# Score matmuls of the first two batches read queries from the transpose buffer, with less bias, and loads and mixing in a new order

## The chip, the cores and the metric

The kernel runs on one core of a Trainium2 chip. The metric is device time in microseconds (us) of one execution. The profile adds a trace of one execution, whose span is about 2 us shorter than the time of the same execution. Engine names are those of the profile: PE is TensorE, PEld its weight loads, DVE is VectorE, ACT is ScalarE, POOL is GpSimd and SP is SyncE.

## The reference, cut to what matters

```python
# batch 8, heads 8, sequence 576, head_dim 64, 8 global tokens, window 32
scores = scale * (q @ k.T)
mask   = (abs(i - j) <= 32) | is_global[i] | is_global[j]
x      = softmax(where(mask, scores, -1e9)) @ v          # heads side by side: [B, 576, 512]
h      = relu(x.T @ w_tok1) @ w_tok2                     # token mixer, 576 -> 256 -> 576
u      = x + h.T
out    = u + relu(u @ w_ch1) @ w_ch2                     # channel mixer, 512 -> 1536 -> 512
```

Each batch therefore goes through scores, exponentials, the rows of the global tokens ("og" in the kernel), the banded product with V ("pv"), the token mixer ("a1p", "hp") and the two channel matmuls ("b1p", "op"). The channel mixer is most of the work of PE.

## The kernel before

K and Q of four heads arrive as 32-row blocks. DVE transposes them into `kcs` and `qcs`, in natural order of the tokens. A copy then spreads each into a layout with one block for each tile of 128 tokens, with 8 columns of the global tokens ahead of each block of queries. The score matmuls read that second layout. In batches 0 and 1 the band mask is added by matmuls of a bias (`biasm`) into the same PSUM tile. Later batches multiply the exponentials by a 0/1 mask (`bandm`) on DVE.

```python
def Xq(b, hg):                       # transpose into natural order
    nc.vector.transpose(out=qcs[hg][:, 0:S]..., in_=st[b]["q16"]...[:, hg]...)

def Xc(b, hg, eng):                  # the copy of Q into blocks with the global columns
    o = qTs[b % 2][:, hg].rearrange("p (t x) -> p t x", t=NT)[:, :, NG:QS]
    copy(eng, o, qcs[hg].rearrange("p (t x) -> p t x", t=NT))

def S_mm0(b, hg, part, rp, ps):      # one score tile: 2 heads
    qf, kT = q16s[b][:, hg], k16s[b][:, hg]
    for i in range(2):
        for off, c0, n in B_SEG[part]:                    # bias
            nc.tensor.matmul(ps[:, i, off:off+n], lhsT=identS, rhs=biasm[:, c0:c0+n], start=(off == 0), stop=False)
    for off, kc, lo, n in S_SEG[part]:                    # 16 matmuls of Q and K
        for e in range(2):
            for i in range(2):
                rs = slice(32 * (2 * rp + i), 32 * (2 * rp + i) + 32)
                nc.tensor.matmul(ps[:, i, off:off+n], lhsT=kT[rs, kc:kc+P, e], rhs=qf[rs, lo:lo+n, e], ...)

# V of batch 0: one block v16 that DVE transposes, four side pieces, and a copy shifted by 32 rows
def load_v0(): ...                                        # v16, 4 transfers
def Xv0(): ...                                            # transpose v16 into vsh
def dup_v(b):
    nc.sync.dma_start(out=vsh[b % 2][32:P, NT:NC], in_=vsh[b % 2][0:P - 32, 2:NT])

def OG(b, get):                                           # rows of the global tokens
    for c in range(NC):
        for r in range(4):
            nc.tensor.matmul(ps[...], lhsT=egs[b % 2][:, c, r], rhs=V[:, c, r::4, :], ...)
    ...                                                   # DVE writes the rows back into V

# --- order of the prologue (cut) ---
eg_const(0); load_v0(); Xk(0, 1); Kc(0, 1, nc.gpsimd)
load_qk(1, (0,)); Xq(0, 1); Xc(0, 1, nc.gpsimd); glob0(1); load_qk(1, (1,))
load_v(0, (0, 5, 6, 7), False)                            # side pieces of V
...
Xv0(); dup_v(0); nc.sync.dma_start(out=vsh[1][0:32, 0:NT], in_=vsh[0][0:32, 0:NT])
...
rest = OG(0, psv)
Xc(1, 0, nc.vector)
S1(0, 0, 0); S1(0, 0, 1); n0 = PV(0, 0, psd); ...         # all four tiles of batch 1, heads 0-3
X1(0, 1, nc.scalar)                                       # K of batch 1, heads 4-7, copied by ScalarE

# --- batch 0: what is mixed with its two channel layers D4 and D5 ---
A = [(0.7, lambda: M2(0, 2, psv))] + s1 + ... + gap(0.8)
A += phase_og(1)[:1] + gap(1.7) + phase_og(1)[1:] + M1u(1)
merge(A, D4[2:])
merge(G(2) + m[:1] + ... + x2[:2] + ... + s2[:1] + x2[2:] + ... + s2[1:] + gap(1.5), D5)
```

`merge` interleaves the pieces of a list with the channel groups by their estimated cost; `gap` holds a place for some microseconds; `fill` puts matmuls on zeros into PE's queue.

The softmax here doesn't subtract the row's maximum and nothing guards it: scores larger than these inputs give would overflow.

Of the kernel before, what the change touches and what calls it, by code (L numbers as in the profile page):

```python
# [17 lines left out]
P = 128  # L18
# [13 lines left out]
B_SEG = (((0, 0, 136), (136, 208, 200), (336, 440, 104), (440, 1088, 72)), ((0, 544, 136), (136, 712, 240), (376, 984, 104)))  # L32
LAG_S = 2
# [3 lines left out]
FILL = (14, 18, 0, 4, 5, 0)  # L37
# [3 lines left out]
def kernel(  # L41
# [236 lines left out]
    def S_mm0(b, hg, part, rp, ps):  # L278
        qf, kT = q16s[b][:, hg], k16s[b][:, hg]
        for i in range(2):  # L280
            for off, c0, n in B_SEG[part]:
                nc.tensor.matmul(
                    ps[:, i, off : off + n], lhsT=identS, rhs=biasm[:, c0 : c0 + n], start=(off == 0), stop=False,
                )
        for off, kc, lo, n in S_SEG[part]:
            for e in range(2):
                for i in range(2):
                    r = 2 * rp + i
                    rs = slice(32 * r, 32 * r + 32)
                    nc.tensor.matmul(  # L290
                        ps[:, i, off : off + n], lhsT=kT[rs, kc : kc + P, e], rhs=qf[rs, lo : lo + n, e],
                        start=False, stop=(e == 1 and off == S_SEG[part][-1][0]),
                    )
# [25 lines left out]
    def S_mask(b, hg, rs=range(4)):  # L319
        for r in rs:  # L320
            eh = e_all[:, 4 * hg + r]
            nc.vector.tensor_mul(out=eh, in0=eh, in1=bandm)  # L322
# [309 lines left out]
    load_qk(0, (1,))  # L632
# [18 lines left out]

    zero_e(e0)
# [4 lines left out]
    zeros(kT3[1].bitcast(F16).rearrange("p g (t x) -> p g t x", t=NT)[:, :, 1:NT, 0 : 2 * WIN])  # L657
    zeros(vsh[0][0:32, 0, :, 0:D])
    zeros(x16s[0][LAST:P, NT - 1])
    zeros(x16s[1][0:LAST, NT - 1])  # L660
# [30 lines left out]
    nc.vector.tensor_scalar(out=ident, in0=it_f[:, 0:P], scalar1=pf, scalar2=None, op0=ALU.is_equal)  # L691
    gidx_f = const.tile([P, NG], F32)
# [5 lines left out]
    for hg in range(2):  # L698
        gather(gq, q, 0, (hg,))
        gather(gk, k, 0, (hg,))  # L700
# [6 lines left out]
    rown, pad = [const.tile([P, NC + 3], F32, name=n) for n in ("rown", "pad")]  # L707
    nc.vector.tensor_scalar(out=pad, in0=kpos, scalar1=-500.0, scalar2=NEG, op0=ALU.is_lt, op1=ALU.mult)
# [4 lines left out]
    nc.vector.tensor_scalar(out=identS, in0=it_f[:, 0:P], scalar1=pf, scalar2=sc, op0=ALU.is_equal, op1=ALU.mult)  # L713

    hgp = int_op("hgp", 4, ALU.logical_shift_right, 1, ALU.bitwise_and)
    nc.vector.tensor_scalar(out=dsel, in0=it8[:, 0:2], scalar1=hgp, scalar2=None, op0=ALU.is_equal)
# [6 lines left out]
    def mask_glob(c0, n):  # L723
        nc.vector.tensor_scalar(
            out=win(biasm[0:32, EB * c0 + 8 : EB * c0 + 8 + P], EB, n),
            in0=it_f[0:32, P * c0 : P * (c0 + n)].rearrange("p (t x) -> p t x", x=P),
            scalar1=gppm[0:32], scalar2=hm1[0:32], op0=ALU.is_equal, op1=ALU.add,
        )
# [5 lines left out]
    mask_rows(EB + 168, 96, 0, 8)  # L734
    Xq(0, 0)
    Xk(0, 0)
    for t, o, x0 in ((qcs, qTs[0][:, 0].rearrange("p (t x) -> p t x", t=NT), NG), (kcs, kT3[0][:, 0].rearrange("p (t x) -> p t x", t=NT), WIN)):
        nc.scalar.copy(out=o[:, :, x0:].bitcast(F16), in_=t[0].rearrange("p (t x) -> p t x", t=NT).bitcast(F16))
    mask_glob(0, 2)
    nc.vector.tensor_scalar(  # L740
        out=biasm[0:32, 4 * EB + 8 : 4 * EB + 72], in0=it_f[0:32, 4 * P : S],
        scalar1=gppm[0:32], scalar2=hm1[0:32], op0=ALU.is_equal, op1=ALU.add,
    )
# [4 lines left out]
    )  # L748
    nc.vector.tensor_mul(out=gd, in0=gd, in1=gd)
    nc.vector.tensor_scalar(out=gd, in0=gd, scalar1=1024.5, scalar2=NEG, op0=ALU.is_lt, op1=ALU.mult)  # L750
    for c0, b0, n in ((0, 0, NT), (NT, 2 * EB - NG, NC - NT)):
# [3 lines left out]
        )  # L755
    def eg_const(i):
# [3 lines left out]
    def glob0(hg):  # L760
        gather_t(gq, gqT, 0, slice(hg, hg + 1))
        globals_(0, nc.vector, (hg,))
        gather_t(gk, gkT, 0, slice(hg, hg + 1))
        for part in (1, 0):
            globals_k(0, nc.vector, part, slice(hg, hg + 1))

    zeros(w1l[LAST:P, 0])
    zeros(w1l[0:LAST, 1])
    zeros(w2[:, :, S:])
    glob0(0)  # L770
    for b0, z0, w, c0 in ((2 * EB + 8, 64, P, 2), (2 * EB + 168, 0, 96, 9)):
        nc.vector.tensor_tensor(
            out=win(biasm[:, b0 : b0 + w], EB, 2), in0=nb[:, z0 : z0 + w].unsqueeze(1).to_broadcast([P, 2, w]),
            in1=rown[:, c0 : c0 + 2].unsqueeze(2).to_broadcast([P, 2, w]), op=ALU.add,
        )
    mask_glob(2, 2)
    eg_const(0)
    load_v0()
    Xk(0, 1)
    Kc(0, 1, nc.gpsimd)  # L780
    load_qk(1, (0,))
    Xq(0, 1)
    Xc(0, 1, nc.gpsimd)
    glob0(1)
    load_qk(1, (1,))
    load_v(0, (0, 5, 6, 7), False)
    nc.gpsimd.dma_start(out=w1, in_=moe_w_tok1[0 : S - LAST, :].rearrange("(c p) x -> p c x", p=P))
    for i in range(2):
# [11 lines left out]
    for n in range(4):  # L800
# [5 lines left out]
        if n == 0:  # L806
            zero_e(e_all)
# [170 lines left out]
```

## Time and profile before

The time was 331.89 us, median of two runs (331.49 to 332.29). The profile is of one more execution, of 329.62 us, with a span of 327.8 us at a mean clock of 0.971 (1 is full speed).

A single tile of the trace marks each stage. "M4" is the first full-width matmul of batch 0's first channel layer.

| landmark | before, us |
|---|---|
| og of batch 0 ends | 30.55 |
| first matmul of the token mixer's second half | 46.66 |
| M4 | 55.16 |
| og of batch 2 starts | 97.49 |
| og of batch 3 starts | 134.22 |
| end of the last matmul | 322.82 |

The parts of the profile that bound the kernel are shown in the prediction below. In PE's timeline, a line gives start, duration, engine, source line, operation, output and inputs, sizes and count, and in brackets the idle time before it with what ended it. This is the start of the token mixer's second half in the kernel before:

```profile
46.66 0.38 PE L579 MATMUL hp_0b<-a,w 128*128 128x512 f16 x1 [1.90 <-ACT a L865]
```

PE stands for 1.90 us until ScalarE has done a ReLU, and 0.35 us more for the other half, which DVE does.

### The profile page before, as it was taken

The numbers are of one execution on the slowest core, as the hardware profiler recorded it, in microseconds if no ns is written. First come the engines' busy times: TensorE is split into PE (matmuls) and PEld (weight loads), VectorE is DVE, ScalarE is ACT, GpSimd is POOL, SyncE is SP. The second block draws the span as 40 slices with busy tenths as digits, with TensorE's granted clock in tenths as the row PEclk, the third lists the DMA queues.
The fourth block names the chain that finished last, engine by engine and source line by source line (L and its number), as shares of the span: only waits on it lengthen the run. The fifth ranks groups of instructions, "written<-read, shape, count | busy, mean of one in ns | idle before, by whom it ended". The sixth has DMA issues, their size and how long they took to land.

```text
span 327.8 us, 7740 instructions
## 1 busy us (share of the span) xinstructions
PE 299.3 (91%) x3194; PEld 160.7 (49%) x3194; DVE 188.3 (57%) x361; ACT 154.9 (47%) x310; POOL 112.0 (34%) x215
## 2 busy tenths in 40 slices
PE   8852967998989999999999999999999999999993
PEld 3542834663435644554445644544456445444641
DVE  7964365266755748595758376757664766151021
ACT  8880434740654555346544562556346535404600
POOL 8865570001588827421732156124312000000000
PEclk9995699999799999999999999999999999999998
DMA  6699999304399999962997069807910251072022
GB/s 120 91 160 176 172 177 203 70 0 98 64 157 168 101 206 111 149 159 59 119 145 146 2 114 143 225 2 123 139 61 2 64 131 32 0 123 87 2 83 77
DMA packets 68290, 34.92 MB, mean 107 GB/s; under 512 B 54656, under 2 KB 58624, under 8 KB 68256
## 3 DMA queue, kind: packets, MB, share of 16 engines
q0 software_dynamic: 44960, 18.19, 47.5%
q1 hardware_dynamic: 23296, 16.25, 19.0%
q8 instruction: 25, 0.41, 0.5%
q14 instruction: 9, 0.07, 0.1%
HBM read 36.38 MB, written 9.44 MB: 140 GB/s over the span
## 4 chain that ended last, share of the span: by engine, by line
PE 69%; DVE 11%; DMA 6%; POOL 6%; issue 3%; ACT 3%; POOLq 0%; DVEq 0%
PE op L478 22%; PE b1p L452 22%; PE s L273 4%; PE hp L411 4%; PE a1p L395 4%; DVE e_all L322 4%; DMA vsh<-in_v_dram 3%; PE pv L370 3%; DMA q<-in_q_dram 3%; PE b1lp L465 2%; PE pv L373 2%; ACT e_all L303 2%; PE s L290 2%; PE og L338 1%; DVE kc L227 1%
## 5 line engine op out<-in xcount | busy, mean ns | idle before, releaser
L452 PE MATMUL b1p<-uT,wc 128*128 128x512 f16 x376 | 91.7, 379 | 2.8 <-DVE osb L482 1.0
L617 ACT ACTIVATE big<-b1p 128x512 f16<-128x512 f32 x95 | 56.6, 598 | 78.3 <-PE b1p L452 76.1
L478 PE MATMUL op<-big 128*128 128x512 f16 x384 | 92.8, 383 | 0.0
L303 ACT ACTIVATE e_all<-s 128x544 f16<-128x544 f32 (+3 forms) x140 | 58.9, 515 | 52.1 <-PE s L273 37.5
L478 PEld LDWEIGHTS <-big 128*128 128x128 f16 x384 | 35.7, 98 | 40.9 <-issue 1.0
L452 PEld LDWEIGHTS <-wc 128*128 128x128 f16 x376 | 33.4, 97 | 40.2 <-issue 7.0
L117 POOL DMA_DIRECT2D vsh<-in_v_dram x60 | 41.7, 713 | 5.8 <-DMA wc<-in_moe_w_ch_dram 3.7
L322 DVE TENSOR_TENSOR e_all<-e_all,bandm 128x1160 f16<-128x1160 f16 x48 | 33.8, 762 | 14.2 <-ACT e_all L303 14.2
L416 DVE TENSOR_TENSOR u<-x,hp 128x1024 f16<-128x1024 f16 x14 | 17.1, 1220 | 34.2 <-PE hp L411 34.2
L482 DVE TENSOR_TENSOR osb<-u,op 128x512 f32<-128x512 f16 x32 | 21.9, 684 | 25.3 <-PE op L478 25.2
L240 POOL COPY kT<-kc 128x640 int32<-128x640 int32 x13 | 9.4, 723 | 78.3 <-DVE kc L227 42.2
L382 DVE TENSOR_TENSOR x<-pv,rr 128x512 f16<-128x512 f32 (+1 forms) x40 | 27.6, 691 | 1.5
L328 POOL COPY eg<-e_all 128x160 f16<-128x160 f16 (+1 forms) x24 | 7.4, 339 | 55.9 <-DVE e_all L322 55.9
L370 PEld LDWEIGHTS <-e_all 128*128 128x128 f16 (+1 forms) x280 | 18.0, 98 | 5.2 <-issue 1.3
L227 DVE STREAM_TRANSPOSE kc<-k 128x576 int32<-128x576 int32 x16 | 19.9, 1244 | 0.4 <-DMA k<-in_k_dram 0.4
L370 PE MATMUL pv<-vsh,e_all 128*128 128x66 f16 (+1 forms) x280 | 20.0, 193 | 0.0
L233 DVE STREAM_TRANSPOSE qc<-q 128x576 int32<-128x576 int32 x16 | 19.8, 1237 | 0.0
L411 PE MATMUL hp<-a,w 128*128 128x512 f16 x72 | 19.1, 379 | 0.6 <-DVE u L416 0.6
L273 PEld LDWEIGHTS <-kT 32*128 32x128 f16 x768 | 12.6, 94 | 14.1 <-issue 11.2
L344 DVE TENSOR_TENSOR vsh<-og,dsel 32x132 f16<-32x132 f32 x32 | 9.2, 288 | 17.6 <-PE og L338 17.2
L381 DVE RECIPROCAL rr<-pv 128x8 f32<-128x8 f32 (+1 forms) x40 | 7.9, 198 | 19.7 <-PE pv L373 16.0
L273 PE MATMUL s<-qT,kT 32*128 32x104 f16 (+3 forms) x768 | 16.3, 218 | 3.1 <-POOL qT L240 2.3
(150 smaller groups left out, 330.3 us busy)
## 6 DMA issues: line engine op xcount, KB each, us to landing
out_dram<-osb SPq DMA_DIRECT2D x32, 256.0 KB, 2.6
k<-in_k_dram POOLq DMA_DIRECT2D x16, 288.0 KB, 9.2
q<-in_q_dram POOLq DMA_DIRECT2D x16, 288.0 KB, 8.2
vsh<-in_v_dram POOLq DMA_DIRECT2D x36, 96.0 KB, 5.5
vsh<-vsh SPq DMA_DIRECT2D x8, 297.0 KB, 6.5
wc<-in_moe_w_ch_dram POOLq DMA_DIRECT2D x3, 512.0 KB, 7.0
big<-in_moe_w_ch_dram POOLq DMA_DIRECT2D x3, 512.0 KB
out_dram<-osb SPq DMA_DIRECT2D x8, 128.0 KB, 5.8
```

The lines of the kernel that those rows point to most:

```text
L117: nc.gpsimd.dma_start(out=V[p0:p1, c, :, 0:D], in_=v[b, :, j0 : j0 + p1 - p0, :].rearrange("h p d -> p h d"))
L227: nc.vector.transpose(out=kcs[hg][:, WIN : WIN + S].rearrange("p (i r) -> p r i", r=RK), in_=st[b]["k16"].bitcast(I32)[:, hg].rearrange("p ...
L273: nc.tensor.matmul(tiles[r // 2][:, r % 2, off : off + n], lhsT=kT[rs, kc : kc + P, e], rhs=qf[rs, lo : lo + n, e], start=(e == 0), stop=( ...
L303: nc.scalar.activation(out=o, in_=i, func=AF.Exp, scale=scale)
L322: nc.vector.tensor_mul(out=eh, in0=eh, in1=bandm)
L370: nc.tensor.matmul(o[0:m], lhsT=e[:, h, c0 : c0 + m], rhs=vs[:, tau, h, :], start=True, stop=(tau == NT - 1))
L382: nc.vector.tensor_tensor(out=x16[r, tau, :].rearrange("p (f h x) -> p f h x", f=2, h=4), in0=pq[r, :, :, 0:D], in1=rr[r].unsqueeze(3).to_ ...
L411: nc.tensor.matmul(ps[:, i, :], lhsT=w2[:, ch, P * tau - sh : P * tau - sh + P], rhs=s["a1"][:, ch, :], start=(ch == 0), stop=(ch == 1),)
L452: nc.tensor.matmul(ps, lhsT=wc1[:, cc, P * j : P * j + P], rhs=s["uT"][:, :, cc, :], start=(cc == 0), stop=(cc == 3))
L478: nc.tensor.matmul(ps, lhsT=w, rhs=wc2[:, j, :], start=(j == 0), stop=(j == NJ - 1))
L482: nc.vector.tensor_add(out=osb, in0=s["u16"][:, tau], in1=ps)
L617: nc.scalar.activation(out=st[b]["b1"][:, j, :], in_=ps, func=AF.Relu)
```

## The change

The intent is to shorten what comes before the steady part: V of batch 0 is loaded ahead of K and Q of batch 1; the score matmuls of batches 0 and 1 read queries from the transpose buffer itself, so that the copies `Xc` go; the bias is added only in 10 of their 16 tiles, and the others are masked after the exponential; batch 2's transposes and scores are mixed into batch 0's channel layers as in the later batches. Because the global columns do not stand in the transpose buffer, each matmul over them and their neighbours is split in pieces. A tile then has 36 or 32 matmuls for Q and K, where it had 16. The diff, cut to its core:

```diff
+def pieces(off, lo, n):              # splits [lo, lo+n) at the global columns
+    ...
-    def S_mm0(b, hg, part, rp, ps):
+    def S_nat(b, hg, part, rp, get, bias):
+        q2, kT = qcs[hg]..., k16s[b][:, hg]
+        gl = gqT...[:, 0, hg, 16 * b : 16 * b + 16]...
+        if bias: ...
         for off, kc, lo, n in S_SEG[part]:
+            seg = pieces(off, lo, n)
             for e in range(2):
+                for o, g, x, w in seg:
+                    for i in range(2):
+                        nc.tensor.matmul(ps[:, i, o:o+w], lhsT=kT[rs, kc:kc+P, e], rhs=(gl if g else q2)[rs, x:x+w, e], ...)
+        S_exp(b, hg, part, rp, ps)
 ... (constants moved on DVE and ScalarE; K's copy of heads 0-3 ahead; FILL changed)
+    gather(gk, k, 0, (0,)); gather(gq, q, 0, (0,))
+    nc.gpsimd.dma_start(out=s["q16"][:, 1], ...)
+    load_v0()
+    gather(gk, k, 0, (1,)); gather(gq, q, 0, (1,))
 ...
+    S_nat(0, 0, 0, 0, pss, False); S_nat(0, 0, 0, 1, pss, False)   # no bias
+    S_nat(0, 0, 1, 0, psv, True)
+    Xq(0, 1); glob0(1); globals_k(1, nc.vector, 1)
+    S_nat(0, 0, 1, 1, pss, True)
+    load_v(0, (0, 5, 6, 7), False)
+    load_qk(1, (0,))
 ...
     def S1(hg, part, rp):
+        S_nat(1, hg, part, rp, pss, hg == 0)
 ...
+    for r in range(4):                 # mask of the unbiased tiles of batch 0
+        ... nc.vector.tensor_mul(out=e0[:, r, c0:c1], in0=e0[:, r, c0:c1], in1=bandm[:, c0:c1])
 ... (in the ladder after og)
-    X1(0, 1, nc.scalar)
+    Xk(1, 1); Kc(1, 1, nc.vector)
-    nc.vector.tensor_scalar_max(out=a1[:, 1], in0=pa[:, 1], scalar1=0.0)
+    nc.scalar.activation(out=a1[:, 1], in_=pa[:, 1], func=AF.Relu)
     M2t(3, hb[:, 1])
-    S1(0, 1, 1)                        # fourth score tile, between the pv products
+    S1(0, 1, 1)                        # the same tile, behind token matmuls
 ... (batch 0)
-            A += phase_og(1)[:1] + gap(1.7) + phase_og(1)[1:] + M1u(1)
+            A += gap(3.5) + phase_og(1)[:1] + gap(1.7) + G(2) + weave(phase_og(1)[1:] + M1u(1), X_units(2))
             merge(A, D4[2:])
-            merge(G(2) + m[:1] + ... + x2[2:] + ... + s2[1:] + gap(1.5), D5)
+            merge(mix(phase_m(1), phase_s(2)), D5)
```

## The prediction

> **What bounds the kernel now.** I read the page first, in its 40 slices of 8.2 us:
>
> ```profile
> PE   8852967998989999999999999999999999999993
> PEclk9995699999799999999999999999999999999998
> ```
>
> TensorE (PE) is busy nearly everywhere from slice 7 on. The holes are in slices 2 to 7 (16 to 60 us) and slice 9, and the granted clock drops just after them (slices 3 and 4, then slice 10). So I cut the span at PE landmarks and asked for busy time by stretch; columns are PE, PEld, DVE, ACT and POOL busy us, then clock, DMA share and GB/s:
>
> ```profile
> 12.00:22.00 10.00, 8.65 (x180) 7.04 (x177) 7.59 (x22) 8.91 (x22) 7.98 (x14) 1.00 0.87 131
> 22.00:29.48 7.48, 0.01 (x2) 0.04 (x2) 3.60 (x7) 1.55 (x3) 2.56 (x4) 0.74 1.34 188
> 29.48:40.00 10.52, 9.15 (x146) 7.78 (x148) 4.40 (x11) 3.36 (x8) 6.66 (x10) 0.54 1.47 169
> 40.00:55.16 15.16, 10.40 (x110) 6.16 (x105) 8.99 (x18) 5.70 (x9) 6.94 (x14) 1.00 1.22 183
> 55.16:93.67 38.51, 35.71 (x432) 19.27 (x432) 21.76 (x43) 20.33 (x44) 9.46 (x15) 0.96 0.49 72
> 93.67:132.32 38.65, 36.82 (x409) 19.58 (x408) 24.92 (x42) 18.32 (x38) 26.14 (x48) 1.00 1.11 152
> 132.49:165.05 32.56, 31.74 (x353) 15.76 (x352) 23.06 (x36) 16.91 (x35) 12.08 (x24) 1.00 0.74 121
> 165.05:200.50 35.45, 35.45 (x405) 19.14 (x405) 22.02 (x35) 17.87 (x37) 13.26 (x30) 1.00 0.71 109
> ```
>
> From 132 us on the kernel is steady: 32.56 us for an even batch, 35.45 for an odd one, PE full. The change leaves the program there as it is, so nothing can be won there. Batch 0 (38.51) and batch 1 (38.65) run longer than their steady kin, and before batch 0's full-width channel matmuls at 55.16 us lies a prologue in which PE waits for long. The waits of the first 60 us and the chain that ended last name the largest hole:
>
> ```profile
> PE og L338 <- DMA vsh<-in_v_dram: 8.1, 1, 8.1
> 17.99 11.35 DMA vsh<-in_v_dram
> ```
>
> The global rows (og) of batch 0 wait for four loads of V that POOL issues at 17.99 to 20.56 us. POOL's timeline shows why so late, and PE's timeline what follows:
>
> ```profile
> 11.58 2.39 POOL L108 DMA_DIRECT2D v<-in_v_dram  x4
> 16.95 0.56 POOL L145 DMA_DIRECT2D k<-in_k_dram  x1
> 17.99 2.57 POOL L117 DMA_DIRECT2D vsh<-in_v_dram  x4
> 13.03 0.62 PE L282 MATMUL s<-biasm,identS 128*128 128x136 f16 x8
> 13.59 0.64 PE L290 MATMUL s<-qT,kT 32*128 32x136 f16 x16
> 32.88 1.03 PE L290 MATMUL s<-qT,kT 32*128 32x136 f16 x16 [1.37 <-DVE qT L242]
> 82.33 0.64 PE L273 MATMUL s<-qT,kT 32*128 32x136 f16 x32 [1.91 <-POOL qT L240]
> ```
>
> V stands behind all of batch 1's K and Q (4 x 288 KB). At 32.88 the same score group takes 1.03 us instead of 0.64: the clock is halved after the hole. At 82.33 PE waits again, for batch 2's K and Q transposes.
>
> **What the Trainium skill says.** "TensorE: Matmul & The Clock Gate", "What's actually happening", has an idle window of about 3.4 us halve the clock and a busy one restore it, in free-running windows. The trace agrees: cut finely, the clock falls at about 25.6 us, in the 8.1 us hole, and returns near 39.25; it falls again for about 3.4 us after the smaller hole at 80.4 to 82.3. The same page, "Wait — 56ns, not 53.3ns?", gives a floor near 25 ns between starts of small matmuls; the narrowest regular stream here, the 66-column pv matmuls, steps by 0.03 us, so nothing contradicts it, but no 8-column matmul runs before the change. "DMA: Bandwidth & Descriptors", "Issuing engines are not separate DMA queues", has all issuers share 16 engines; the 11.35 us of the V load among batch 1's traffic, against a median of 5.5 us for that group, agrees.
>
> **The change, part by part.**
>
> *Loads.* In program order V (the v16 block and the four side pieces) now comes before batch 1's K and Q; Q of heads 4 to 7 moves behind the first two gathers. POOL, added up with the durations of before: first gathers at about 6.5 us (the indices come some 0.4 us later, as four small DVE operations go ahead of them), Q at 8.8, v16 from 9.4 to 11.8 (before 11.58 to 13.97), two gathers to 14.3, one K copy of 0.72, V pieces from 15.0 to 17.6: 3 us earlier, with no batch 1 traffic ahead. I expect them landed by about 22 (before 29.34).
>
> *Then another input is last.* The transposed v16 must be copied to the shifted rows by one more DMA, which took 7.1 us before (issue 21.4). On DVE the transpose now comes after all bias work and both glob copies; adding DVE's operations from 7.1 us (Xk 1.1, Xq 1.1, gathers' wait to 10.6, bias 0.6 + 0.75 + 0.75, Xk and Xq 2.2, globals 1.0, band mask 0.7) puts it at 17.7 to 19.8. So the copy lands near 27. The last eg copy also waits: it stands behind Xk of batch 1, now loaded after V (about 23 to 24 us), and behind the last exp at about 25. I put og's end at 27.6, against 30.57.
>
> *Scores.* Splitting a group at the global columns turns 16 matmuls into 36 (part 0) or 32 (part 1). Columns stay equal. With two row groups, an extra 8-column matmul should cost about 25 ns (an estimate from the pv step of 30 ns and that page's floor): 0.5 us a tile in part 0, 0.4 in part 1. Over 16 tiles: 8 x 0.5 + 8 x 0.4 = 7.2 us. Bias is dropped in 6 tiles (2 of batch 0, 4 of batch 1): 44 matmuls at 0.62/8 = 0.077 us, 3.4 us back. Net PE work +3.8 us, but of that +3.4 falls in batch 0's tiles, inside the old hole (tiles end near 24 instead of 21.4, og comes later anyhow); batch 1's four tiles of heads 0 to 3 cost +1.8 on the path, and its other four gain about what they lose.
>
> *Copies gone.* The Q copies of batches 0 and 1 vanish (0.80 us DVE and 1.37 us of PE waiting at 32.9; 1.26 us ACT twice). The DVE masking added for unbiased tiles (about 2.1 us in batch 0, 4 x 0.76 in batch 1) lies beside PE.
>
> *Prologue sum.* og end 27.6; score tile to 29.2; V rows ready at 29.2 (DVE chain 1.4 us, as before); two pv to 30.3; tile to 31.9; two pv to 32.9; tile to 34.3; token matmuls and last pv to 37.1, which was 44.6 before. Then the ladder of small steps to the first full-width channel matmul took 10.6 us; about 1.4 go with the ACT copy that stood in it, and one score tile (1.4 on PE, partly hidden) comes in: 10. That is 47.1. But between 24 and 27.2 PE does little, and I give 65% to another halving of the clock, worth about 2.2 us: 48.5 against 55.16, so **-6.7**.
>
> *Batch 0, from there.* The steady kin less two channel groups already done is 32.56 - 1.8 = 30.8; four score tiles near 1.05 add 4.2: 35.0. To reach it, batch 2's transposes must be ready when the second layer starts, and the new program does place them in the first layer, with scores mixed as in steady state. 35.0 against 38.51: **-3.5**.
>
> *Batch 1.* Its loads of batch 3 and gathers are still issued in a burst after batch 0's last group, so it stays above 35.45. I take 37.5: **-1.2**.
>
> Sum: 331.9 - 6.7 - 3.5 - 1.2 = **320.5 us**.
>
> **Rivals.** (1) *A new wait eats the V gain.* og still needs the shifted copy and, through DVE's order, K of batch 1. For it: five DMAs now compete while the copy runs; DVE is in order. Against: the copy is issued some 1.5 us earlier and V is off the path. If it lands at 29.5, the prologue gains only about 4: total 323 to 325. (2) *The extra matmuls cost more*, say 50 ns each, weight loads included: 288 x 25 ns more is 7 us, of which some 4 are on the path: 324 to 325. Against: the 32-row group in steady state steps by 20 ns a matmul with four row groups. (3) *DVE becomes the bound in batch 0's first layer*: masks, transposes, norms and og sum to about 16 us, in some 17 us. Then 2 us are lost: 322 to 323. (4) *No halving at all*: 2 us better, 318.
>
> **Range and chances.** The prologue may give 3.5 to 9.5, batch 0 1.5 to 4.5, batch 1 -0.5 to 2.5. These partly add, giving 315 to 327. Missing 2% (6.6 us) takes two of rivals 1 to 3 at once. Faster by over 2%: 0.86; within: 0.12; slower: 0.02, as nothing reaches the steady part.
>
> **What would show each step.** og's start near 26 to 27 us, its last releaser a DMA of vsh from vsh rather than from V; V pieces issued near 15 us. Score groups of 36 at about 1.05 us full clock (50 ns more each: rival 2). Clock 0.5 in one or two windows after og, not four. First full-width channel matmul at 48.5 +- 3. The wait for batch 2's Q copy (1.91) gone, no half clock near 84, batch 0's stretch near 35. Batches from 2 on at 32.6 and 35.5. The prediction fails if og starts after 29, or if POOL's queue makes batch 1's K late.

## The result

The changed kernel took 322.98 us, median of two runs (322.65 to 323.3). The ratio of its time to the time before is 0.9731, with a 95% interval of 0.9666 to 0.9797. Ratios here are the mean time of one kernel's runs over that of the other's of the same rounds, so they are not quite the ratio of the medians quoted. When the same kernel was timed again on another chip (first experiment), it took 320.09 us, with a ratio of 0.9667. The span of the first profile was 321.4 us at a clock of 0.965.

The first stage, then batch 0, then batch 1, then the first steady batch, of the changed kernel; columns are as in the prediction:

```profile
0.00:51.87 51.87, 40.61 (x665) 28.08 (x665) 33.47 (x111) 28.45 (x59) 33.62 (x67) 0.80 1.08 153
51.87:87.22 35.35, 32.57 (x477) 17.12 (x476) 25.28 (x44) 19.30 (x42) 9.30 (x16) 1.00 0.72 107
87.22:125.16 37.94, 36.60 (x410) 19.42 (x409) 23.53 (x40) 18.18 (x37) 25.21 (x46) 1.00 1.03 141
125.16:157.50 32.34, 31.10 (x349) 15.42 (x347) 22.42 (x36) 16.50 (x34) 11.71 (x21) 1.00 0.75 122
```

The prologue fell from 55.16 to 51.87 (-3.3), batch 0 from 38.51 to 35.35 (-3.2) and batch 1 from 38.65 to 37.94 (-0.7). The rest of the span grew by 0.8 us, from 195.5 to 196.2, so the sum is the 6.4 us between the spans. Clock by slice, from the page:

```profile
PEclk9955799999999999999999999999999999999998
```

The half clock near 84 us is gone. In the prologue, however, the clock is low from slice 3 on, earlier than before: cut finely, it is at 0.50 from 15.6 to 36.1 us, where that had been 25.6 to 39.2.

How og of batch 0 ran, in PE's timeline:

```profile
27.48 0.74 PE L357 MATMUL og<-vsh,eg 128*32 128x132 f16 x20 [1.04 <-ACT big L322]
30.61 0.52 PE L357 MATMUL og<-vsh,eg 128*32 128x132 f16 x12 [2.39 <-DMA vsh<-vsh]
```

The releaser is no longer a load of V but the shifted copy (vsh from vsh), as was foreseen; but og ends at 31.13 us, later than the 30.55 of before. To see why, one goes back along the copy, through the timelines of POOL, of DVE and of SP's queue:

```profile
9.53 2.30 POOL L120 DMA_DIRECT2D v<-in_v_dram  x4
12.13 1.02 POOL L211 DMA_INDIRECT gk<-in_k_dram,idx_i  x1 [0.30 <-issue]
...
15.17 2.04 POOL L129 DMA_DIRECT2D vsh<-in_v_dram  x3
```

```profile
18.29 0.21 DVE L217 STREAM_TRANSPOSE gkT<-gk 128x32 int32<-128x32 int32 x1 [3.43 <-DMA gk<-in_k_dram,idx_i]
...
20.22 2.13 DVE L139 STREAM_TRANSPOSE vsh<-v 128x512 int32<-128x512 int32 x2
```

```profile
22.45 0.62 SPq L134 DMA_DIRECT2D vsh<-vsh  x1
```

The V pieces were issued at 15.17 us, as predicted. But the gathered keys of heads 4 to 7, issued at 12.13 right behind the block v16, landed only at 18.29. DVE works in order and waited 3.43 us for them. V's transpose stood behind it, ended at 22.35, and the shifted copy was issued at 22.45 and landed at 30.47, 8.0 us later.

After og the changed kernel is faster. The line that answers to the wait of 1.90 us shown before is now:

```profile
42.90 0.86 PE L598 MATMUL hp_0b<-a,w 128*128 128x512 f16 x2 [0.69 <-ACT a L887]
```

From og's end to this matmul it is now 11.8 us, where it was 16.1. And at the place where PE waited 1.91 us for batch 2's queries, there is no wait left:

```profile
72.43 0.64 PE L285 MATMUL s<-qT,kT 32*128 32x136 f16 x32
```

### The profile page after: what moved, and what is told of

The parts are those of the page before. It is cut to its first block, busy times and chain, and to the rows that moved or that the text cites. A ratio compares the mean times of both kernels' runs of the same rounds, so it can differ in the third digit from the quotient of the medians.

```text
span 321.4 us, 8239 instructions
## 1 busy us (share of the span) xinstructions
PE 299.0 (93%) x3436; PEld 161.3 (50%) x3436; DVE 189.2 (59%) x364; ACT 152.6 (47%) x309; POOL 110.6 (34%) x214
## 4 chain that ended last, share of the span: by engine, by line
PE 70%; DMA 13%; DVE 9%; issue 3%; ACT 2%; POOL 1%; DVEq 0%; ACTq 0%; SPq 0%
PE b1p L471 25%; PE op L497 19%; PE a1p L414 4%; DMA uT<-u 4%; DMA out_dram<-osb 4%; PE hp L430 4%; PE b1lp L484 3%; DVE e_all L341 3%; PE pv L389 3%; PE s L285 3%; DMA vsh<-vsh 2%; PE pv L392 2%; DMA v<-in_v_dram 2%; PE s L308 2%; PE og L357 1%
## 5 line engine op out<-in xcount | busy, mean ns | idle before, releaser
L497 PE MATMUL op<-big 128*128 128x512 f16 x384 | 91.8, 380 | 0.0
L497 PEld LDWEIGHTS <-big 128*128 128x128 f16 x384 | 35.5, 98 | 40.5
L471 PEld LDWEIGHTS <-wc 128*128 128x128 f16 x376 | 33.4, 97 | 40.7 <-issue 6.5
L341 DVE TENSOR_TENSOR e_all<-e_all,bandm 128x1160 f16<-128x1160 f16 x52 | 36.5, 757 | 17.3 <-ACT e_all L322 17.3
L252 POOL COPY kT<-kc 128x640 int32<-128x640 int32 x14 | 10.3, 733 | 64.9 <-DVE rr L400 56.3
L347 POOL COPY eg<-e_all 128x160 f16<-128x160 f16 (+1 forms) x24 | 6.4, 295 | 67.5 <-DVE e_all L341 67.5
L401 DVE TENSOR_TENSOR x<-pv,rr 128x512 f16<-128x512 f32 (+1 forms) x40 | 27.6, 691 | 1.6
L392 PE MATMUL pv<-vsh,e_all 128*128 128x66 f16 x224 | 17.2, 193 | 0.0
L308 PE MATMUL s<-gqT,kT 32*128 32x8 f16 x256 | 14.1, 175 | 3.2 <-DVE gqT L217 2.3
```

Source lines behind the costliest of these rows:

```text
L308: nc.tensor.matmul(ps[:, i, o : o + w], lhsT=kT[rs, kc : kc + P, e], rhs=(gl if g else q2)[rs, x : x + w, e], start=(e == 0 and o == off a ...
L341: nc.vector.tensor_mul(out=eh, in0=eh, in1=bandm)
L392: nc.tensor.matmul(o, lhsT=e[:, h, c1 : c1 + P], rhs=vs[:, NT - 1 + tau if tau else 1, h, :], start=False, stop=True)
L401: nc.vector.tensor_tensor(out=x16[r, tau, :].rearrange("p (f h x) -> p f h x", f=2, h=4), in0=pq[r, :, :, 0:D], in1=rr[r].unsqueeze(3).to_ ...
L471: nc.tensor.matmul(ps, lhsT=wc1[:, cc, P * j : P * j + P], rhs=s["uT"][:, :, cc, :], start=(cc == 0), stop=(cc == 3))
L497: nc.tensor.matmul(ps, lhsT=w, rhs=wc2[:, j, :], start=(j == 0), stop=(j == NJ - 1))
```

## The experiments

**The theory**: (a) V's move gave nothing, as the shifted copy and the exponentials then end last; (b) the gain of the prologue is in the ladder after og, where copies left the path; (c) the extra small matmuls cost PE little; (d) the half clock in the prologue is off the path; (e) batch 0's gain is the new mixing. **The rivals:** V's order is what gains; the missing half clock or the missing bias is; the extra matmuls are dear and hide a larger gain.

All kernels gave correct results. Each was timed in three rounds, and the kernel before ran beside it (its medians were 330.15 to 330.9). Runs of one call share a chip: the first four; the next four; the next three; the last alone. The landmarks come from one profile each, and those of the same kernel differ: 50.95 to 51.87 for M4, and 318.8 to 321.4 for the span, in the two profiles of the changed kernel. Up to M4, merge_old, merge_old2 and bias_b1 are the changed kernel too, and with them M4 lies between 50.37 and 52.80. A difference at M4 of less than 2.4 us, read from one profile each, is therefore within what the same program shows. M4 to og 2 is steadier: 38.64 to 38.66 in the six profiles that have the changed kernel's program there. The two ratios of the changed kernel, 0.9731 and 0.9667, differ by 0.6% with overlapping intervals; the others are to be held against both.

| kernel | og 0 ends | M4 | M4 to og 2 | og 2 to og 3 | median us | ratio to before (95%) |
|---|---|---|---|---|---|---|
| before | 30.55 | 55.16 | 42.33 | 36.73 | 331.89 | 1 |
| changed, first | 31.13 | 51.87 | 38.65 | 36.86 | 322.98 | 0.9731 (0.9666-0.9797) |
| after_again | 29.91 | 50.95 | 38.66 | 35.33 | 320.09 | 0.9667 (0.9610-0.9724) |
| merge_old | 29.92 | 50.69 | 45.07 | 36.67 | 329.76 | 0.9976 (0.9916-1.0036) |
| xv0_first | 29.82 | 50.80 | 38.64 | 36.14 | 320.73 | 0.9691 (0.9635-0.9747) |
| dup_copy | 28.30 | 50.01 | 38.64 | 35.35 | 320.41 | 0.9677 (0.9618-0.9735) |
| merge_old2 | 29.68 | 52.80 | 42.65 | 38.42 | 326.80 | 0.9915 (0.9857-0.9973) |
| bias_b1 | 29.61 | 50.37 | 38.85 | 36.58 | 321.72 | 0.9745 (0.9702-0.9787) |
| warm | 29.60 | 50.68 | 39.27 | 36.58 | 323.14 | 0.9786 (0.9736-0.9835) |
| b_nat1 | 29.95 | 53.23 | 43.22 | 37.39 | 330.12 | 0.9996 (0.9952-1.0041) |
| b_vfirst | 30.38 | 56.91 | 42.00 | 37.00 | 330.21 | 1.0002 (0.9965-1.0040) |
| post_old | 29.56 | 54.50 | 38.64 | 35.33 | 323.39 | 0.9795 (0.9757-0.9832) |
| best2 | 26.69 | 50.03 | 38.64 | 35.32 | 319.24 | 0.9670 (0.9634-0.9705) |
| split2 | 35.7 | 61.07 | 44.08 | not read | 338.06 | 1.0224 (1.0155-1.0294) |

### after_again: the changed kernel once more

No edit. Expected:

> Control: the changed kernel again, beside which the others of this call are read. Both theories: 323 us, give or take 0.6, ratio to the kernel before 0.973.

Measured: 320.09 us (319.31 to 320.86), span 318.8. Against the kernel before, M4 came 4.2 us earlier, M4 to og 2 was 3.7 shorter, og 2 to og 3 was 1.4 shorter and the rest 0.5 longer. It follows that the first profile was a slightly slower run of the same thing: 0.9 us of the 2.6 between the two spans lie before M4 and 1.5 in batch 1. Before M4, og already ended 1.2 us earlier here: DVE waited 2.77 us for the gathered keys instead of 3.43, and the shifted copy took 7.5 us instead of 8.0. This run is the control for what follows.

### merge_old and merge_old2: the mixing of batch 0 undone

```diff
 # merge_old: gap(0.8) and the old lists; merge_old2: the same lists behind gap(3.5)
-            A += gap(3.5) + phase_og(1)[:1] + gap(1.7) + G(2) + weave(phase_og(1)[1:] + M1u(1), X_units(2))
-            merge(mix(phase_m(1), phase_s(2)), D5)
+            A += phase_og(1)[:1] + gap(1.7) + phase_og(1)[1:] + M1u(1)
+            merge(G(2) + m[:1] + ... + x2[:2] + ... + s2[:1] + x2[2:] + ... + s2[1:] + gap(1.5), D5)
```

> The changed kernel with one part undone: the order in which batch 2's transposes and scores are merged into batch 0's channel layers is again that of before. Theory (the new order is what shortened batch 0's stretch from 38.5 to 35.4 us): 2.5 to 3.5 us slower than the control, so about 326, and TensorE waits again for batch 2's Q copy with a half clock after it. Rival (the stretch shortened because four score tiles lost their bias matmuls, 28 x 0.077 = 2.2 us): at most 1 us slower than the control.

> As merge_old, but og of batch 1 keeps its new, later place; only batch 2's transposes, its global copies, its V load and the mixing of its scores go back to the old order. merge_old lost 9.7 us, more than the 2.5 to 3.5 expected, and its trace shows TensorE waiting 2.8 and 2.3 us about og of batch 1. Theory (two separate losses: og asked for too early for the new masks, about 4 us; and batch 2's transposes late, about 4 us): 4 to 5.5 us slower than the control of the first call (ratio to the kernel before near 0.981), the 2.8 us wait about 1.1 again, the wait for batch 2's Q copy still there. Rival (og's place does not matter, it all comes from batch 2's transposes): as slow as merge_old, ratio 0.998.

Measured: merge_old 329.76 us, 9.7 us over the control. PE's timeline in merge_old and in merge_old2, at og of batch 1 and at batch 2's first scores:

```profile
59.32 0.64 PE L357 MATMUL og<-vsh,eg 128*32 128x132 f16 x32 [2.81 <-issue]
...
80.89 0.65 PE L285 MATMUL s<-qT,kT 32*128 32x136 f16 x32 [1.91 <-POOL qT L252]
```

```profile
61.19 0.64 PE L357 MATMUL og<-vsh,eg 128*32 128x132 f16 x32 [1.09 <-issue]
...
80.25 0.65 PE L285 MATMUL s<-qT,kT 32*128 32x136 f16 x32 [1.92 <-POOL qT L252]
```

Merge_old2 took 326.80 us, and its ratio of 0.9915 lies between the two expectations (0.981 and 0.998). With the old lists the wait for POOL's copy of batch 2's queries is back, at 1.91 and 1.92 us. It is only a part of the loss: M4 to og 2 is 4.0 us longer in merge_old2 (42.65 against 38.66). The other part is the half clock, which is back too, from 81.4 to 84.8 us: PE is busy for 37.26 us of this stretch instead of 35.43, with about the same matmuls (489 and 491 records). Placing og of batch 1 early costs 2.4 more (45.07); PE waits 2.81 us ahead of it instead of 1.09. Batch 1 is 1.3 to 3.1 us longer as well, but the 3.1 comes from the slowest of merge_old2's four runs (329.71). So the new mixing is worth more here than the whole saving that I had put down to batch 0. Merge_old (0.9976) is not quite the order of before: it has the masks of the change, and the score tiles keep the new cost estimates (0.6 instead of 1.2). How much of the change would be left with the true old order was not run.

### xv0_first and dup_copy: V's chain shortened

```diff
 # xv0_first: V's transpose ahead of the gathers of heads 4-7
     Xq(0, 1)
+    Xv0()
     glob0(1)
 ...
-    Xv0()
     dup_v(0)
```

```diff
 # dup_copy: the shifted copy by three copies on DVE, without a DMA
-    dup_v(0)
+    for p0 in (0, 32, 64):
+        nc.vector.tensor_copy(out=vsh[0][p0+32:p0+64, NT:NC]..., in_=vsh[0][p0:p0+32, 2:NT]...)
```

> VectorE transposes the v16 block before the global rows and columns of heads 4 to 7, so it does not stand behind the gather it waited 3.4 us for. Theory (og's end is set by the shifted copy of V, which is issued when this transpose ends): the copy is issued near 20 instead of 22.5 us and lands near 28 instead of 30.6; 1.5 to 2.5 us faster than the control. Rival (the last exponentials and the eg copies are as late, 27.7 us, and get later by 1 to 2 us as tiles of heads 4 to 7 start later): at most 0.7 us faster.

> The shifted copy of V for batch 0 is made by three VectorE copies of 32 rows (about 0.95 us each, as the same size took) instead of one DMA of 8 us. Theory (that DMA is the last thing og waits for): og ends near 28.5 to 29 instead of 31.1, 1.5 to 2.5 us faster than the control. Rival (VectorE in order is the true limit, its 2.9 us of copies push masks, transposes and the eg copies back by as much): within 0.7 us of the control.

Measured: 320.73 and 320.41 us, against 320.09 of the control. In xv0_first the copy was issued at 19.68 us, where the prediction had it. Og in xv0_first, and then in dup_copy:

```profile
28.64 1.18 PE L357 MATMUL og<-vsh,eg 128*32 128x132 f16 x32 [1.04 <-ACT big L322]
```

```profile
27.23 1.07 PE L357 MATMUL og<-vsh,eg 128*32 128x132 f16 x32 [1.41 <-ACT big L322]
```

V is no longer last in either. ScalarE's last exponentials are, and og ends at 29.82 and 28.30. So two chains end close together before og, and shortening V's chain alone gains 0.1 to 1.6 us at og, at most 0.9 at M4 and nothing in the time that these runs can tell; in both, the rival of the expectation was right. A part of what is lost may be the clock. The last exponentials wait for score tiles, which PE runs at 0.50 from about 15 us on in both kernels. In dup_copy, PE has no wait from og to 40 us, but stays at 0.50 until 35.6, 7.3 us past og, where it was 3.5 us in the control.

### b_vfirst: V's order alone, in the kernel before

```diff
     Kc(0, 1, nc.gpsimd)
+    load_v(0, (0, 5, 6, 7), False)
     load_qk(1, (0,))
 ...
-    load_v(0, (0, 5, 6, 7), False)
```

(K and Q of batch 1, heads 4 to 7, follow directly on those of heads 0 to 3.)

> The kernel before, with one part of the change alone: the four V side pieces of batch 0 are issued ahead of batch 1's K and Q. Theory (og would then wait for the shifted copy, issued at 21.4 us and 7.1 us long): V lands by about 23 instead of 29.3, og starts near 28.5 instead of 29.5, 0.5 to 1.5 us faster in the prologue, and not more than 1 us in the time. Rival (the V load is the whole of the 8.1 us hole): og starts near 24 and the kernel gains 4 us or more.

Measured: 330.21 us, ratio 1.0002. The side pieces of V were issued at 15.22 us, where it had been 17.99; og then waited for the shifted copy, as the timeline of PE shows:

```profile
26.57 0.74 PE L338 MATMUL og<-vsh,eg 128*32 128x132 f16 x20 [3.01 <-DVE eg L328]
29.86 0.52 PE L338 MATMUL og<-vsh,eg 128*32 128x132 f16 x12 [2.54 <-DMA vsh<-vsh]
```

Og ended at 30.38 us, against 30.55. M4 even came 1.75 us later (56.91); the clock stayed at 0.50 until 44.7 us there. The part of the change that I had held to be worth most is worth nothing by itself.

### post_old: two steps of the ladder after og undone

```diff
     S1(0, 1, 0)
+    S1(0, 1, 1)
     pa = pss(...)
 ...
-    Kc(1, 1, nc.vector)
+    Kc(1, 1, nc.scalar)
 ...
     M2t(3, hb[:, 1])
-    S1(0, 1, 1)
```

> The changed kernel with two placements of before: the fourth score tile of batch 1's heads 0 to 3 goes back ahead of the token matmuls, and the K copy of its heads 4 to 7 goes back to ScalarE, where it stood ahead of the token activations. Theory (the prologue won its 3 to 4 us after og, from end of og to the first channel-mixer matmuls 16.1 us before against 12.0 in the control, by these two and by the lost Q copy): 1.5 to 2.5 us later at the first full-width channel matmul than the control's 50.95, and 1 to 2.5 us slower in time. Rival (only the lost Q copy did it): within 0.7 us of the control at that point.

Measured: 323.39 us, ratio 0.9795, its interval clear of the control's (0.9667), but not of the first measurement's (0.9731, up to 0.9797). M4 stands at 54.50, 3.55 us later than in the control, though og ends at 29.56. Both are more than expected. The wait for the ReLU is back in part:

```profile
45.58 0.97 PE L598 MATMUL hp_0b<-a,w 128*128 128x512 f16 x2 [1.69 <-ACT a L888]
```

Not all of the 3.55 us need come from the order. The clock was at 0.50 until 39.4 us (33.4 in the control), and again from 46.2 to 49.7, after this wait. In merge_old2, which has the changed kernel's program up to M4, it was at 0.50 until 40.5, and M4 stood at 52.80. So 1.7 us (54.50 against 52.80) are the least that can be put down to the two steps and to the half clock behind the wait, and 3.55 the most: the fourth score tile behind token matmuls, and K's copy off ScalarE. The two were not separated.

### b_nat1: the Q copies of batch 1 removed, in the kernel before

```diff
 # S1 uses S_nat(1, hg, part, rp, pss, True); these go:
-            Xc(1, hg, eng)
-    globals_(1, nc.vector)
-    Xc(1, 0, nc.vector)
```

> The kernel before, with one part of the change alone: batch 1's scores take queries in natural order (bias kept in all tiles, loads and order as before), and batch 1's Q copies and global Q copies go. Theory (the added narrow matmuls are nearly free: the trace of the changed kernel has 36 in 0.6 us where 16 took 0.6; the Q copy on VectorE and TensorE's 1.37 us wait for it go, and a ScalarE copy of 1.26 us): 1 to 2.5 us faster than the kernel before. Rival (each costs 25 ns as predicted, 144 x 25 ns = 3.6 us): 1 to 2 us slower.

Measured: 330.12 us, ratio 0.9996, so neither expectation held. M4 came 1.9 us earlier (53.23), of which 0.6 is an earlier og; but M4 to og 2 took 0.9 us and og 2 to og 3 0.7 us more, and the last matmul ended at 322.89 against 322.82. The start of the token mixer still waits 1.91 us for ScalarE.

Taking the copies alone thus gives something early and it is lost again. By which mechanism it is lost was not settled.

### bias_b1: the bias of batch 1's heads 4 to 7 back

```diff
-        S_nat(1, hg, part, rp, pss, hg == 0)
+        S_nat(1, hg, part, rp, pss, True)
 ... (and the DVE masking of these heads removed)
```

> The changed kernel, with the bias matmuls back in the four score tiles of batch 1's heads 4 to 7 and the VectorE masks for them gone. Theory (TensorE is the bound there): 28 bias matmuls x 0.077 = 2.2 us more on TensorE, and 1.5 to 2.2 us slower. Rival (VectorE's masks, 4 x 0.76 us, are what og of batch 1 waits 1.1 us for): no slower, or up to 1 us faster.

Measured: 321.72 us, ratio 0.9745 (0.9702 to 0.9787); the intervals overlap with the control's, so the total does not settle it. The stretch that holds these tiles is 38.85 us against 38.66, so 0.2 us longer. The reason can be read from PE's waits up to 55 us in the changed kernel:

```profile
PE s L308 <- ACT e_all L322: 0.7, 1, 0.7
```

These tiles wait for ScalarE's exponentials to free a PSUM tile. In bias_b1, which has more PE work there, this wait is not listed: from M4 to og 2 PE is busy for 37.41 us instead of 35.43, and the 2.0 us more fill time in which it had been waiting.

### warm: matmuls on zeros to hold the clock up

```diff
-    fill(FILL[1])
+    fill(12)
     S_nat(0, 0, 0, 0, pss, False); S_nat(0, 0, 0, 1, pss, False)
+    fill(6)
 ... (fill(8) after batch 0's fourth score tile, fill(10) ahead of og, 10 more inside og)
```

> The changed kernel with idle matmuls on zeros added in TensorE's holes of the prologue (4 more at the start, 6 and 8 between score tiles, 10 before og, 10 inside og where it waits for the shifted copy), so that the granted clock should not fall. Theory (the halved clock from about 16 to 35 us costs time only after og, since og waits for the shifted copy in any case: two score tiles and pv at half speed, some 2.5 us): 1.5 to 3 us faster than the control, clock 1.00 through the prologue. Rival (the fills themselves hold up the score tiles, or the steps after og wait on VectorE anyway): within 1 us of the control.

Measured: 323.14 us, ratio 0.9786, its interval (0.9736 to 0.9835) clear of the control's but not of the first measurement's. It is not faster, as the theory had it, and probably slower. The clock row of warm shows that the fills did what they were for:

```profile
PEclk9999999899999999999999999999999999999998
```

Yet M4 came at 50.68, and in the control, with a clock of 0.50 from 19.7 to 33.4 us, at 50.95. In warm the first 20 matmuls of og start at 26.14 us without a wait, but the others end at the old time, since the copy has not landed:

```profile
26.14 0.47 PE L359 MATMUL og<-vsh,eg 128*32 128x132 f16 x20
29.24 0.36 PE L359 MATMUL og<-vsh,eg 128*32 128x132 f16 x12 [0.37 <-DMA vsh<-vsh]
```

After og, at full clock, PE then waits twice where the control doesn't wait, 1.06 us for V's rows from DVE and 1.04 us without a releaser. So a half clock that lasts 3.5 us past og, as in the control, is hidden behind other waits. A longer one is not. Merge_old2 has the same program up to M4, and its clock stayed at 0.50 from 13.1 to 40.5 us. These lines give the stretch from og's end to the same token matmul, in merge_old2 and then in the control; columns are as in the prediction:

```profile
29.68:40.81 11.13, 11.13 (x201) 9.27 (x201) 5.81 (x14) 3.36 (x8) 3.47 (x5) 0.52 1.42 198
29.91:38.97 9.06, 8.19 (x203) 7.06 (x201) 5.73 (x14) 3.11 (x8) 3.47 (x5) 0.81 1.22 207
```

PE never waits there in merge_old2, and takes 2.1 us longer; from this matmul to M4 the two need the same 12.0 us. The half clock in the prologue is thus worth from about nothing to 2.1 us, by how long it lasts after og, and part (d) of the theory holds only for a short one. What sets its length was not found: the same program had it end at 33.2 to 40.5 us. Why warm is slower by about 3 us in the medians is only in part located: its profiled run, 1.1 us longer than the control's, loses 0.6 us between M4 and og 2, where its clock is at 0.50 from 55.2 to 58.5, and 1.2 between og 2 and og 3.

### split2: every piece of a score matmul cut in two

```diff
-    return out
+    return [h for o, g, x, w in out for h in ((o, g, x, w // 2), (o + w // 2, g, x + w // 2, w - w // 2))]
```

The tiles of part 0 then have 72 matmuls for the same columns.

> The disputed cost by itself: in the changed kernel every piece of the scores of batches 0 and 1 is cut in two (8 columns into 4 and 4, 128 into 64 and 64), so a part 0 tile has 72 matmuls instead of 36, with the same columns. The changed kernel's trace has 36 in 0.6 us where 16 took 0.57 to 0.6. Theory (a floor holds for each row group, and two groups run side by side; the first doubling hid beside columns and weight loads, the second will not): 72 x 25 / 2 = 0.9 us a tile, and the kernel slower by 1 to 2.5 us, as part of the tiles wait on ScalarE anyway. Rival A (a floor of 25 ns for the engine as a whole, as the prediction took it): 1.8 us a tile, over 6 us slower. Rival B (only columns count): 0.6 us a tile, the time of the control.

Measured: 338.06 us, ratio 1.0224, some 18 us over the control of the first call. The theory had expected 1 to 2.5 us more; for the time, the rival that said over 6 is the nearer. For one tile, the theory was right (0.9 us). At full clock a tile without bias takes about 0.93 us (62.03 to 62.96) for its 72 matmuls, 13 ns each, where the changed kernel takes 0.60 us for 36 (52.83 to 53.43), 17 ns each. The starts in the trace show the floor that the theory spoke of: the two row groups start mostly 3 to 12 ns apart, and within one row group a start follows the last by mostly 25 to 30 ns, for 4 columns as for 64. That is 0.33 us more a tile, or 5 us for 16 tiles if all of it lay on the path, and so not the greater part. Where the rest goes is seen in PE's waits up to 75 us, in split2 and then in the control's waits from 28 to 52 us; columns are us in total, times, and the longest:

```profile
PE s L308 <- issue: 7.1, 6, 2.8
PE pv L389 <- issue: 2.1, 1, 2.1
PE s L297 <- issue: 1.9, 1, 1.9
```

```profile
PE s L308 <- issue: 0.9, 1, 0.9
```

"Issue" means that PE waited for nothing that the profile shows, neither a semaphore nor a transfer. The waits fall in the middle of tiles:

```profile
27.13 0.24 PE L297 MATMUL s<-biasm,identS 128*128 128x104 f16 x1 [1.91 <-issue]
33.33 0.23 PE L308 MATMUL s<-qc,kT 32*128 32x48 f16 x3 [2.58 <-issue]
40.61 0.24 PE L389 MATMUL pv<-vsh,big 128*128 128x66 f16 x1 [2.06 <-issue]
```

Counted in the trace, 128 matmuls lie between the first and the second of these waits and 127 between the second and the third; to the next long one, at 67.73 us, there are 511, four times 127.75. A matmul comes with one weight load, so 128 matmuls are 256 instructions. The Trainium skill, "Runtime: NRT & Kernel Launch", "Instruction fetch mechanics", says that an engine's instructions come in blocks of 16 KiB, 256 instructions, over a DMA queue of its own, and that the cost of crossing a block is "mostly hidden". The spacing agrees with the block, and so does the queue that carries instructions (q8 on the page): it has 31 packets in split2 and 27 in the control. Four packets more for 544 matmuls more (3980 against 3436), which is 1,088 instructions or 4.25 blocks of 256. Ahead of each of these waits' ends, one packet of that queue starts at 24.8, 31.0, 38.4 and 65.4 us, and PE goes on 2.2 to 2.3 us later. Other runs fit: waits of this kind stand after 478 matmul records in the control, in merge_old and in bias_b1, after 479 and 607 in split2 and after 351 and 605 in warm. These counts are equal to within 2 or 126 to 128 apart, though what stands at them differs (score tiles, a bias matmul, a pv product). The profile's busy share of the DMA engines is 1.15 from 20 to 30 us and 1.34 from 30 to 40. I read this as PE waiting for instructions. The counts and the packets support it, but no run changed the supply alone, so it is the best reading and not shown by an intervention. These waits sum to 11.1 us. The remainder is the longer tiles and, in part, the clock, which is at 0.50 from 20 to 40 us and again below 1.00 between 60 and 80; the two were not separated.

This also puts a limit on the finding that extra small matmuls are free: the control, at 18.3 matmuls a microsecond from 10 to 40 us, works near the 17 to 21 that split2 got from one such wait to the next (128 in 6.2 us, 127 in 7.3, of which 1.03 us was a wait for DVE), and it has one wait of this kind, of 0.87 us.

### best2: the pieces that looked useful, together

```diff
+    gather(gk, k, 0, (1,)); gather(gq, q, 0, (1,))      # ahead of v16
     load_v0()
 ... (masks of batch 0 ahead of V's transpose; shifted copy by DVE as in dup_copy;
      the zero rows of the other V buffer by a GpSimd memset; fills 12, 6, 3, 6)
```

> A version meant to beat both: the changed kernel, with the gathers of heads 4 to 7 issued ahead of the v16 block, the masks ahead of the v16 transpose, the shifted copy as three VectorE copies, the DMA that seeds the other V buffer from this one (which the trace shows VectorE waiting for at 30.4 us before it may write og's rows) replaced by a GpSimd memset, and a few idle matmuls to keep the clock. Theory (in the prologue og and what follows wait for those two copies of 8 us and for the gather behind v16): og ends near 25 to 26 instead of 29.9, the first full-width channel matmul starts 3 to 5 us earlier than the control's 50.95, and the time falls to 316 to 317.5. Rival (the chain after og is bound by other loads or by VectorE, as warm, xv0_first and dup_copy gained next to nothing): at most 1 us gained.

Measured: 319.24 us (318.75 to 319.5), ratio 0.9670. It beats the kernel before; against the changed kernel (0.9667 and 0.9731) nothing is separated, and the 316 to 317.5 us of the theory were missed. With the gathers ahead of v16, DVE had the keys of heads 4 to 7 at 14.71 us without a wait, which confirms what had held it. Og ended at 26.69, 3.2 us earlier than in the control, but M4 came only 0.9 us earlier. PE's timeline shows what took the place of V:

```profile
26.05 0.64 PE L357 MATMUL og<-vsh,eg 128*32 128x132 f16 x32 [2.91 <-POOL vsh L830]
28.33 0.18 PE L308 MATMUL s<-gqT,kT 32*128 32x8 f16 x2 [1.08 <-DVE kT L233]
29.49 0.29 PE L308 MATMUL s<-qc,kT 32*128 32x128 f16 x2 [0.98 <-DVE qc L245]
```

Og waits for POOL, whose memset of V's zero rows (a part of this version) ran from 22.50 to 25.11 us; then the score tiles behind og wait for batch 1's K and Q on DVE. An earlier og is therefore followed by the next chain within 2.3 us. From 29.5 to 40 us PE then has no wait, but its clock is at 0.50 from 28.6 to 35.4, which takes a further part of the gain.

## Why the prediction was right or wrong, point by point

The total was right: 320.5 us predicted, 322.98 and then 320.09 measured, faster by more than 2%. Its parts, -6.7, -3.5 and -1.2, stand against -3.3, -3.2 and -0.7 in the first profile, and against -4.2, -3.7 and -1.4 in the control (where the last two are read between M4, og 2 and og 3).

1. **V and og: the step that failed** is "I put og's end at 27.6". It ended at 31.13, and at 29.91 in the control. POOL's part was right to 0.5 us (V pieces from 15.17 to 18.1; 15.0 to 17.6 predicted). Wrong was DVE: "adding DVE's operations" (the listed ones add to 16.6 us, not to the 17.7 given) left out that the gathers of heads 4 to 7, issued behind 512 KB of v16, would hold DVE until 18.29. V's transpose began at 20.22 instead of 17.7, and the copy took 8.0 us instead of 7.1: together the 3.5 us of the first profile. The assumed "last exp at about 25" was early too, as it ended at 27.65 and, in the control, at 26.15; xv0_first and dup_copy show that it would have been the next bound. For V alone, 17.7 was about the earliest possible, since in xv0_first DVE waits for the block v16 until 17.50. This was the first rival, which I had described and put at 323 to 325. The sign of failure that I had given, og starting after 29, did not catch it, since og started at 27.48 and stopped midway.
2. **After og: right in the sum**, and it is where the gain was. From og's end to M4 the sum gave 20.9 us (1.4 of them for the clock); it was 20.7, and 21.0 in the control, against 24.6 before. Post_old shows that two reorderings in this ladder, with the half clock that came with them, make 1.7 to 3.55 us of the gain. A shorter half clock may be another part: it lasted 8.7 us past og before, and 5.0 and 3.5 us in the two profiles of the changed kernel. With 10.8 us, in merge_old2, og to M4 took 23.1, so that 1.5 us of the 3.9 are left. The whole miss of the prologue (M4 at 51.87 instead of 48.5) is as large as og's.
3. **The half clock: right in size only when long.** "I give 65% to another halving of the clock, worth about 2.2 us" was 1.4 us of the sum. The halving came, and lasted 3.5 us past og in the control, but warm, without it, reaches M4 just 0.3 us earlier. Where it lasted 10.8 us past og, in merge_old2, it cost 2.1 us. As the sum after og fits for the control only with the 1.4 us in it, other steps cost more than I gave them, and that they made up for each other is luck: in the control the token matmuls end 10.5 us after og (9.5 predicted), and the ladder behind them takes 10.5 (10 predicted).
4. **The extra matmuls: mis-sized as to PE.** "0.5 us a tile in part 0": a tile of 36 took 0.60 us from start to start, where one of 16 took 0.56 (13.59 to 14.15). The sum of 7.2 us in all was near nothing. Its split was also wrong: of the net 3.8 us, 2.4 and not 3.4 fall in batch 0 by the prediction's own terms (3.6 of matmuls less 1.2 of bias). Rival 2 (50 ns each) is dead for this count; split2 shows a limit of another kind at twice the count.
5. **The bias: mis-sized.** Batch 1's four tiles without it were to gain about what their extra matmuls lose. They gain 0.2 us for the four and lose next to nothing: the 2.0 us of PE work that the bias takes go into time in which PE otherwise waits, for ScalarE among others.
6. **Batch 0: right** (-3.5; measured -3.2), and mainly for the reason given: merge_old2 loses 4.0 us in this stretch, with the wait of 1.9 us for the Q copy back, and the half clock. The sum that gave 35.0 was in part luck. It had four tiles at 1.05 us, which took 0.60 us each and so 1.8 less, and no waits; but PE was idle for 2.8 us of the 35.35, as it had been of the 38.51. The wait for the Q copy went, others came, such as 1.1 us ahead of og. That og's place in it is worth another 2.4 us was not in the prediction.
7. **Batch 1: right on average, and uncertain.** 37.5 predicted, 37.94 in the first profile. Og 2 to og 3 takes either 35.3 us or 36.1 to 36.9 in kernels that have the same program there; in the slower ones a channel group waits some 0.8 us for ACT or DVE. What decides between the two is open.
8. **Steady part: right.** 32.34 us for the first even batch, 32.56 predicted.

Rival 3 (DVE bound in batch 0) showed little: PE's waits for DVE between M4 and og 2 sum to at most 1.5 us. Rival 4 (no halving) brought 0.3 us of M4 in warm. The total stayed well inside the range because og's miss of 2.3 to 3.5 us is the only large one: no other stage missed by more than 0.8 us in the first profile.

## What to carry to other kernels

Before crediting an earlier load, follow its data through every in-order queue up to the consumer: here a small gather, queued behind a large block, held DVE and with it V. In a prologue several chains end within 1 to 2 us of each other, so the gain of one is what remains until the next, and the steps behind the wait (copies on the engine that also does the ReLU, the place of independent matmuls) may hold more than the wait itself. When one kernel's profiles differ at a landmark, compare their clocks there first: a half clock that is hidden behind waits in one run can stand on the path in the next. Cutting matmuls finer cost little at 36 in a tile and much at 72, where PE, as far as the trace can be read, waits for its instructions.

## What the Trainium skill lacked or had wrong

- "TensorE: Matmul & The Clock Gate", "Wait — 56ns, not 53.3ns?": its floor near 25 ns between starts is given for the engine, without row groups. Here it held for each 32-row group, with starts mostly 25 to 30 ns apart in split2, while two groups ran side by side: 36 matmuls took 0.60 us, a mean of 17 ns, and in split2 72 took 0.93 us, a mean of 13 ns. (The part of that page on packing small matmuls has row groups run at the same time, but doesn't take up the floor.)
- "Runtime: NRT & Kernel Launch", "Instruction fetch mechanics": fetching is called mostly hidden. With streams of matmuls this small and the DMA engines full, waits of 1.91, 2.58 and 2.06 us without a semaphore stand 128 and 127 matmuls apart in split2 (the cause is a reading, see there). I found no rate there at which an engine outruns its supply; here, at half clock and with the DMA engines busy, PE got about 17 to 21 matmuls with their weight loads a microsecond.
- "DMA: Bandwidth & Descriptors": I found no figure there for what a small gather takes behind a large block. Here it took 6.2 us from issue (12.13) to use (18.29), and the SBUF-to-SBUF copy of 297 KB took 8.0 us.
- "TensorE: Matmul & The Clock Gate", "What's actually happening": nothing there is wrong here, but it doesn't say when a half clock costs time. In the control 13.7 us at 0.50 before M4 cost 0.3 us against warm, which had none; in merge_old2, with 27.3 us at 0.50, the same program reached M4 1.85 us after the control. (The penalty that the page's "Terms" give, half of the throttled time, would be an estimated 6.8 us for each of these two steps, so here it is a bound and not the loss.)
